# An E-Branchformer layer, forward and backward, on one core: one instruction plan for the whole program in place of three, a new table of order offsets, and the last weight loads issued by another engine

## The chip, the cores and the metric

The kernel runs on one core of a Trainium2 chip. The metric is device time in microseconds (us), lower is better. The core's engines are TensorE (PE: matmuls, with PEld for loading the stationary operand), VectorE (DVE), ScalarE (ACT), GpSimd (POOL) and SyncE (SP), which here only issues DMA transfers. Each engine works through its own instructions in a fixed order and waits by semaphores where it needs another's result.

## The reference

One layer on x of shape (B, T, D) = (2, 4000, 144), and then its gradient with respect to all inputs; `_gelu` is the tanh form, `_layernorm` has no weights:

```python
    xa = _layernorm(x)
    q, k, v = split(xa @ w_qkv)
    p = softmax(q @ k.T * D ** -0.5)
    glob = (p @ v) @ w_att_out
    h = _gelu(xa @ w_mlp_in);  u, g = split(h);  g = _layernorm(g)
    gc = depthwise convolution of g over 5 time steps by dw_csgu
    loc = (u * gc) @ w_mlp_out
    m = concatenate([glob, loc]);  m = m + depthwise convolution of m over 5 time steps by dw_merge
    out = x + m @ w_merge
    # outputs: out, and the gradients of x, w_qkv, w_att_out, w_mlp_in, dw_csgu, w_mlp_out, dw_merge, w_merge for grad_out
```

Outputs are named `out_0` (the layer's result), `out_1` (the gradient of x) and `out_2` to `out_8` (of the weights).

## The kernel before

**Rows.** Nearly all of the time goes to attention, forward and backward at once, in `phase_att` (line 1525), called once per batch. A batch's 4000 tokens are 32 row blocks of 125. Below, "row" means such a block, 0 to 31 for the first batch and 32 to 63 for the second. For one row the steps are:

- `jit_mm`, `jit_tr` (lines 1574 to 1602): the row's queries and its output gradient, folded with the weights, are made by matmuls, copied to `qz` and transposed into `qt` by a DMA transpose (L1597).
- `quad` (from line 1606): scores **S** of the row against all 4000 tokens, and **dP** (gradient times values) for the row before it, in four quarters. A quarter has 128-row matmuls of 500 columns (L1615) and remainder matmuls with 16 rows (L1621), into PSUM tiles `ps`, of which there are two.
- `S_min` (VectorE, L1639): copy of the scores to `Pb` with the running extreme for the softmax; `P_exp` (ScalarE, L1647) the exponential; `P_tr` (L1651) one DMA transpose of the row's whole P, issued by SyncE, `SX<-Pb`.
- `PdP` (L1657, or L1660 and L1662): P times dP, into `SX`; `st_half` (L1844): its transpose in two DMA transposes by SyncE, `SX<-SX`.
- **Y** (`Y_half`, L1671): 32 matmuls from the transposed P into the row's attention result; **Z** (`Z_half`, L1717): 32 matmuls from the transposed P times dP. Both go to a PSUM tile `yz`, of which there is one. Y and Z are written to DRAM (`Yn_d`, `Zn_d`), and Z's row is transposed into `zt` (L1731).
- **X** (`X_group`, L1762): matmuls that add the parts for keys and values of all 32 blocks, two rows at a time, from `Pb` and `SX`; VectorE adds them up in `acc` (L1766, L1768).

For the last row of a batch the transposes are done by TensorE (`last_tr`, L1707). Between these steps lie the pieces of the local branch (`local_units`, line 450).

**Head.** Ahead of and inside the first two rows the class `Head` builds folded weights and `pre_pieces` the normalised input `xa_aug` and its transpose `xaT_m`; its `rstd` is a power on GpSimd (L399), and the taps of the depthwise convolutions are multiplied out on GpSimd (L236). A tile of zeros is written to DRAM (`zdram`) to fill padding.

**Boundaries.** At the end of a batch the class `Merge` loads `go_h` and `Yg` (L2003, L2004, L2017, L2018 and the helper lines 41 and 42), and runs the merge branch's matmuls `Hmm` (`Hps`, L2053). The first boundary, between the batches, lies near 540 to 590 us of the profile, the second, before the weights' gradients (class `Final`), near 1150 to 1220.

**Weights for the end.** `end_weights` (line 98) loads the weights that `Final` and the last steps of `Merge` use into a space where the data `goT` and `xaT_m` were. Its DMAs are issued by GpSimd; it is called after the second batch's rows, and the planner places its loads where the space is free.

**What sets the order.** The program is written in source order. The class `Planner` (line 1104) then orders each engine's instructions by a simulated list schedule. Each instruction group has a key: its place in the source plus an offset from the table `LEAD`, which is looked up by its class (the step's tag, the engine, the tile's name, as in `H15t P` or `e_gn D.rsr`). At each simulated moment the ready group with the lowest key is taken, no further than 700 instructions ahead of the oldest that is left. Costs of instructions and DMAs are formulas in `cost` and `plan`. `plan` is called three times: twice from `phase_att`, when t reaches the last row of a batch, and at the end. So the order of each engine is three plans, one after the other: nothing crosses a cut.

Of the kernel before, what the change touches and what calls it, by code (L numbers as in the profile page):

```python
# [14 lines left out]
D = 144  # L15
# [82 lines left out]
def end_weights(k, W, pool):  # L98
    eng = k.nc.gpsimd
    W.Wqkv = load_k_(k, pool, k.w_qkv, 0, 3 * D, "Wqkv_e", eng)  # L100
    W.Wo = load_k_(k, pool, k.w_att_out, 0, D, "Wo_e", eng)
    W.Wm = [load_k_(k, pool, k.w_merge, h * D, D, "Wm_e%d" % h, eng) for h in range(2)]
    W.Wl = load_k_(k, pool, k.w_mlp_out, 0, D, "Wl_e", eng)
    W.Wvo = unspill(k, pool, W.Wvo_d, "Wvo_e", eng)
    W.sWm = [unspill(k, pool, W.sWm_d[h], "sWm_e%d" % h, eng) for h in range(2)]
    W.sWr = [unspill(k, pool, W.sWr_d[h], "sWr_e%d" % h, eng) for h in range(2)]


class Head:
# [18 lines left out]
    def loads(self):  # L128

        k, W, nc, wp, wt = self.k, self.W, self.k.nc, self.k.wpool, self.wt  # L130
        k.PL.tag("hl")
# [313 lines left out]
U0 = 1  # L445

# [251 lines left out]
Fdwct A.Pb:-15251 D.Pb:-13343 D.jf:1333 P:-5943 S.out_5_dram:-14635  # L698
Fdwit A.Pb:2718 D.Pb:-11748 P:-17532 S.out_4_dram:-14282
Fdwm0t A.Pb:-15906 D.Pb:-5467 D.dwma:-18911 D.jf:-15667 P:-12424 S.out_8_dram:-19182  # L700
Fdwm1t A.Pb:-19065 D.Pb:-16718 D.dwma:-19949 D.jf:-17808 P:-13749 S.out_7_dram:-14976 S.out_8_dram:-17102
Fdwvt A.Pb:-12429 P:-17392 P.Pb:-11874 S.out_2_dram:-13890 S.out_3_dram:-20599
Fdwxt A.Pb:-11921 P:-16236 P.Pb:-16679 S.out_6_dram:-16186
Fhbt A.Pb:-16772
Fht0t A.Pb:-15071 P:-16732 P.Pb:-15290
Fht1t A.Pb:-5982 P:-13475 P.Pb:-6001
Fqkt A.Pb:-5046 D.Pb:1780 P:-19513 P.Pb:-14575 S.out_2_dram:-12213
Fweightst A.Pb:2012 A.R:-11583 D.R:-12504 P:-16671 P.Pb:4074
H0d P:3856
H0t P:2300  # L710
H10d P:3336
H10t P:1535
H11d P:1114
H11t P:-15701
H12d P:-577
H12t P:-14835
H13d P:4246
H13t P:2042
H14d P:-996
H14t P:-12628  # L720
H15d P:-2292
H15t P:-19983
H1d P:1355
H1t P:-18472
H2d P:-10611
H2t P:-11591
H3d P:-2204
H3t P:2819
H4d P:-3689
H4t P:-15136  # L730
H5d P:-11610
H5t P:-16462
H6t P:-17582
H7d P:143
H7t P:2736
H8d P:1402
H8t P:4559
H9d P:-828
H9t P:-10610
clrh D.qz:121  # L740
da0d D.dx_s:1989 D.pj:1819
da0t D.dx_s:-19356 D.pj:4366
da1d D.dx_s:1833 D.pj:-2064
da1t D.dx_s:1450 D.pj:380
da2d D.dx_s:-1184 D.pj:-11591
da2t D.dx_s:-16872 D.pj:-16742
da3d D.dx_s:-9926 D.pj:2641
da3t D.dx_s:1738 D.pj:-14783
da4d D.dx_s:2120 D.pj:-10584
da4t D.dx_s:-14598 D.pj:-13576  # L750
da5d D.dx_s:1764 D.pj:-2040
da5t D.dx_s:-17958 D.pj:-15842
da6d D.dx_s:-26 D.pj:-4981
da6t D.dx_s:-17014 D.pj:167
da7d D.dx_s:-809 D.pj:-1508
da7t D.dx_s:-13863 D.pj:-17458
db0d A.t:1488 D.dx_c:-2255 D.t:-10855 P.Pb:-9933 S.out_1_dram:3805
db0t A.t:-15437 D.dx_c:-4986 D.t:-16936 P.Pb:-14840 S.out_1_dram:-11860
db1d A.t:8260 D.dx_c:593 D.t:-10761 P.Pb:-450 S.out_1_dram:-763
db1t A.t:-14235 D.dx_c:-14619 D.t:-14824 P.Pb:-18556 S.out_1_dram:-4816  # L760
db2d A.t:-10051 D.dx_c:-346 D.t:-1051 P.Pb:1345 S.out_1_dram:-10878
db2t A.t:-14314 D.dx_c:2973 D.t:-14455 P.Pb:-16686 S.out_1_dram:-15013
db3d A.t:-2311 D.dx_c:-12078 D.t:-256 P.Pb:4162 S.out_1_dram:-5923
db3t A.t:5187 D.dx_c:1471 D.t:-14832 P.Pb:-14659 S.out_1_dram:-14078
db4d A.t:700 D.dx_c:-5966 D.t:1978 P.Pb:5255 S.out_1_dram:-1006
db4t A.t:2357 D.dx_c:-15418 D.t:-17568 P.Pb:-16684 S.out_1_dram:3764
db5d A.t:7691 D.dx_c:1168 D.t:3548 P.Pb:4528 S.out_1_dram:1494
db5t A.t:-13237 D.dx_c:-12298 D.t:2401 P.Pb:-18508 S.out_1_dram:-14515
db6d A.t:-1202 D.dx_c:143 D.t:-2913 P.Pb:6516 S.out_1_dram:-1989
db6t A.t:992 D.dx_c:-905 D.t:-16578 P.Pb:-11985 S.out_1_dram:-12231  # L770
db7d A.t:-1326 D.dx_c:-2082 D.t:-2907 P.Pb:-1548 S.out_1_dram:-5951
db7t A.t:3489 D.dx_c:1682 D.t:-12820 P.Pb:-19955 S.out_1_dram:-13857
dgn_un D.c:-1050 D.l_gc:1027 D.nc:-45 P:6418 P.l_w:-5741
dhT_un S.dhT:-9892
dmd A.A_dM1T:3192 P:-1498
dmt D.A_dM1T:-13970 P:1403
dug_un A.dugr:-3801 P:-11295
dug_une A.dugr:3554 P:1368
dug_unh A.dugr:-1398 P:3647
dwc_un0 A.l_fl:-590 P:1255 P.A_dwc:4666  # L780
dwc_un1 A.l_fl:1673 P:-1034 P.A_dwc:4861
dwi_un A.l_fl:-979 P:3938 P.A_dWiT:-5316
e_dgc D.gd:1399 P.gd_rem:-11587 S.gd:-1599
e_dgce D.gd:-3413 P.gd_rem:-4142 S.gd:1142
e_dgch D.gd:1199 P.gd_rem:-11746 S.gd:6998
e_dh D.dhr:-1092 D.l_dd:-12499
e_du D.l_dd:6397
e_gn D.rsr:-2328 P.gd:-3884
e_gne D.rsr:-79 P.gd:7432
e_gnh D.rsr:-303 P.gd:-161  # L790
e_gp D.gpr:3201 D.l_sq:2314
e_gpe D.gpr:-3362 D.l_sq:2278
e_h D.l_hg:1917 P.l_q:-6726
e_he D.l_hg:1135 P.l_q:8342
e_hh D.l_hg:1742 P.l_q:544
e_m D.l_z:6720 P.l_th:-4350
e_me D.l_z:5526 P.l_th:-114
e_mh D.l_z:543 P.l_th:-52
e_stat D.mv:589 D.st:-39 D.ve:-938 P.rsr:1338 P.ur:5433
e_state D.mv:-314 D.st:1383 D.ve:1372 P.rsr:-178 P.ur:-10200  # L800
e_stath D.mv:1805 D.st:-408 D.ve:-4106 P.rsr:-5732 P.ur:-252
e_tanh A.l_th:-10935 D.l_z:-1255 P.l_a:1563
e_tanhe A.l_th:1202 D.l_z:3963 P.l_a:-377
e_tanhh A.l_th:76 D.l_z:406 P.l_a:595
ehd D.Hs:7635 S.H_d:-597
eht D.A_H:-15626
ex0 A.Pb:-2362
ex0d A.Pb:-310
ex0e A.Pb:-2899
ex0h A.Pb:2136  # L810
ex0t A.Pb:-13483
ex1 A.Pb:2211
ex1d A.Pb:-10370
ex1e A.Pb:-931
ex1h A.Pb:-499
ex1t A.Pb:-17638
ex2 A.Pb:2132
ex2d A.Pb:6419
ex2e A.Pb:222
ex2h A.Pb:997  # L820
ex2t A.Pb:2723
ex3 A.Pb:2425
ex3d A.Pb:1449 P:-9919
ex3e A.Pb:-2552
ex3h A.Pb:-9641
ex3t A.Pb:-45 P:-11409
gc_uni A.l_gc:3754 D.ugr:-1884 P:5596 S.ug_d:-6345
gm0d A.goT:-10916 P:-1170
gm0h A.goT:-5942 P:535
gm1d A.goT:-628 P:3264  # L830
gm1h A.goT:-408 P:-942
gm2d A.goT:-1090 P:3249
gm2h A.goT:-7899 P:3264
gm3d A.goT:-466 P:-2130
gm3h A.goT:1016 P:-5787
gmad A.goT:-10233 P:-2750
gmah A.goT:-12011 P:-621
gmbd A.goT:3435 P:-2104
gmbh A.goT:-171 P:-3462
grd P.go_r:3222  # L840
grh P.go_r:-209
gs0d D.R:-4545 P:1256
gs0h D.R:15 P:1219
gs1d D.R:-2449 P:313
gs1h D.R:-12605 P:-10337
gs2d D.R:440 P:-6571
gs2h D.R:950 P:817
gs3d D.R:-1058 P:-835
gs3h D.R:2954 P:-4366
hRh D.R:-4194  # L850
hah P.A_dWiT:-973 P.A_dwc:-11699
# [5 lines left out]
hm1h A.Q:1240 A.RW:127 A.SX:2039 P:4414  # L857
hm1th A.M1T:-8007 P:4192
hoh P.xa_aug:-1937
htapr0h P.SX:1965  # L860
htapr1h P.SX:-1414
htp00h A.SX:-2503
htp10h P.SX:2191
# [1769 lines left out]
```

## Time and profile before

| | us |
|---|---|
| median of 3 runs | 1293.33 (1292.07 to 1297.97) |
| the profiled execution | 1294.54, with a span of 1292.8 |
| mean granted clock of TensorE | 0.996 |
| TensorE busy | 1243.4 (96%) |
| VectorE busy | 1050.1 (81%) |
| ScalarE busy | 756.4 (59%) |
| GpSimd busy | 502.4 (39%) |

The profile's page gives each engine's busy time, the chain that ended last, the costliest groups of instructions with their mean durations, and the DMA queues; busy time of PE comes from modelled ends. The trace behind it was also asked for the busy time by windows, for what an engine waited for, and for the order in time at single places. In such rows `SPq` is SyncE's time for issuing a transfer, and a line such as `DMA SX<-SX` in the chain is a transfer from its issue to its landing.

### The profile page before, as it was taken

How to read it: one execution, taken by the hardware profiler on the slowest of the kernel's cores; microseconds unless marked ns; L12 is line 12 of the kernel's file. 1: busy time of each engine (PE TensorE's matmuls, PEld its weight loads, DVE VectorE, ACT ScalarE, POOL GpSimd, SP SyncE). 2: the span in 40 equal slices, each digit the busy share in tenths (PEclk: the TensorE clock that was granted, in tenths of full speed). 3: DMA queues.
4: the chain of work that ended last, by engine and by line, in shares of the span. 5: the costliest groups of instructions: out<-in, count | busy, mean ns of one | idle time of the engine just before them, and what ended most of it. 6: DMA issues, size and time to landing. Idle time of an engine off the chain costs nothing.

```text
span 1292.8 us, 38682 instructions
## 1 busy us (share of the span) xinstructions
PE 1243.4 (96%) x15698; PEld 1024.7 (79%) x15698; DVE 1050.1 (81%) x2824; ACT 756.4 (59%) x1232; POOL 502.4 (39%) x987
## 2 busy tenths in 40 slices
PE   6999999999999999989899999999999999998998
PEld 3578888888788888879787878888888888886997
DVE  7599888989898988668868988888889798876655
ACT  4766666665666566443846656666666666553382
POOL 7553434334434433313634444444444343331111
PEclk9999999999999999999999999999999999999999
DMA  3588988898889898794259998999799898999612
GB/s 101 105 159 156 161 156 154 142 166 150 155 146 153 154 163 150 135 219 113 67 108 171 152 150 158 163 154 160 136 144 169 150 157 149 168 152 154 158 27 84
DMA packets 631017, 186.50 MB, mean 144 GB/s; under 512 B 611651, under 2 KB 625766, under 8 KB 630832
## 3 DMA queue, kind: packets, MB, share of 16 engines
q1 hardware_dynamic: 629490, 182.39, 78.1%
q8 instruction: 122, 2.00, 0.6%
q0 software_dynamic: 800, 1.44, 0.5%
q14 instruction: 57, 0.47, 0.1%
q10 hardware_dynamic: 548, 0.21, 0.1%
HBM read 20.82 MB, written 14.22 MB: 27 GB/s over the span
## 4 chain that ended last, share of the span: by engine, by line
PE 79%; DMA 8%; DVE 7%; ACT 2%; POOL 2%; issue 1%; SPq 0%; DVEq 0%; POOLq 0%; ACTq 0%
PE X L1762 20%; PE ps L1615 15%; PE yz L1717 10%; PE yz L1671 8%; PE ps L1621 7%; DMA SX<-SX 3%; PE po L2150 2%; PE Hps L2053 2%; DMA SX<-Pb 1%; PE pj L1578 1%; PE pc L581 1%; PE pd L529 1%; PE pd L596 1%; PE pw L641 1%; DMA qt<-qz 1%
## 5 line engine op out<-in xcount | busy, mean ns | idle before, releaser
L1639 DVE TENSOR_SCALAR_CACHE_REDUCE Pb<-ps 125x1000 bf16<-125x1000 f32 x256 | 306.3, 1197 | 74.5 <-PE ps L1621 71.8
L1647 ACT ACTIVATE Pb<-Pb,nm 125x1000 bf16<-125x1000 bf16 x256 | 279.0, 1128 | 119.1 <-DVE nm L1641 118.4
L1762 PE MATMUL X<-SX 125*125 125x144 bf16 x2048 | 294.8, 229 | 2.1 <-ACT l_fl L623 1.9
L1762 PE MATMUL X<-SX,Pb 125*125 125x144 bf16 x2048 | 290.0, 226 | 0.0
L1762 PEld LDWEIGHTS <-SX 125*125 125x125 bf16 x2048 | 259.1, 137 | 28.4 <-issue 28.4
L1660 ACT CAST SX<-ps 125x1000 bf16<-125x1000 f32 x189 | 188.1, 995 | 152.8 <-PE ps L1621 149.2
L1615 PE MATMUL ps<-xaT_m,qt 128*125 128x500 bf16 x1024 | 264.1, 378 | 3.5 <-DMA qt<-qz 1.9
L1762 PEld LDWEIGHTS <-Pb 125*125 125x125 bf16 x2048 | 260.5, 137 | 3.1 <-issue 3.1
L1768 DVE TENSOR_TENSOR acc<-X,acc 125x432 f32<-125x432 f32 x372 | 200.5, 551 | 37.3 <-PE X L1762 34.9
L1717 PE MATMUL yz<-xa_aug,SX 125*125 125x144 bf16 x2048 | 153.5, 230 | 10.9 <-DMA SX<-SX 8.2
L1615 PEld LDWEIGHTS <-qt 128*125 128x125 bf16 x1024 | 122.1, 138 | 43.7 <-issue 2.7
L1717 PEld LDWEIGHTS <-SX 125*125 125x125 bf16 x2048 | 141.2, 139 | 19.1 <-DMA SX<-SX 9.5
L1671 PE MATMUL yz<-xa_aug,SX 125*125 125x145 bf16 x2048 | 142.0, 227 | 1.8 <-DMA SX<-Pb 1.8
L1671 PEld LDWEIGHTS <-SX 125*125 125x125 bf16 x2048 | 135.1, 137 | 3.6 <-DMA SX<-Pb 2.5
L1662 DVE TENSOR_TENSOR SX<-SX,Pb 125x1024 bf16<-125x1024 bf16 x189 | 131.5, 696 | 4.2 <-ACT SX L1660 4.0
L1621 PEld LDWEIGHTS <-qt 16*125 16x125 bf16 x1024 | 37.0, 129 | 102.0 <-issue 102.0
L1621 PE MATMUL ps<-XR,qt 16*125 16x500 bf16 x1016 | 112.2, 421 | 0.0
L1657 DVE TENSOR_TENSOR SX<-ps,Pb 125x1000 bf16<-125x1000 f32 x67 | 80.1, 1195 | 7.9 <-PE ps L1621 6.6
L1695 POOL TENSOR_SCALAR SX<-qz,rl 125x144 bf16<-125x144 bf16 x62 | 25.5, 412 | 146.2 <-DVE rl L1677 123.8
L624 POOL TENSOR_TENSOR A_dwc<-l_fl,A_dwc 128x512 f32<-128x512 f32 (+2 forms) x48 | 38.5, 801 | 102.6 <-ACT l_fl L623 102.4
L499 POOL TENSOR_SCALAR l_a<-l_sq 125x576 bf16<-125x576 bf16 x32 | 22.3, 696 | 106.7 <-ACT l_sq L497 106.4
L2053 PE MATMUL Hps<-Yg,go_h 125*128 125x144 bf16 x640 | 53.8, 226 | 1.7 <-DMA Yg<-ug_d 1.7
(498 smaller groups left out, 2293.7 us busy)
## 6 DMA issues: line engine op xcount, KB each, us to landing
Yn_d<-yn SPq DMA_DIRECT2D x64, 35.2 KB
Zn_d<-qz SPq DMA_DIRECT2D x64, 35.2 KB
ug_d<-ugr SPq DMA_DIRECT2D x32, 70.3 KB
SX<-in_x_dram SPq DMA_DIRECT2D x16, 140.6 KB
out_dram<-Pb SPq DMA_DIRECT2D x16, 140.6 KB
out_dram<-SX SPq DMA_DIRECT2D x16, 140.6 KB
Pb<-in_grad_out_dram SPq DMA_DIRECT2D x8, 252.0 KB
go_h<-in_grad_out_dram SPq DMA_DIRECT2D x4, 504.0 KB
```

The costliest lines, as they stand in the source:

```text
L1615: mm = nc.tensor.matmul(pp[r // 2][:, r % 2, 0:CH], QT[i][:, 3 * h, 0:PB], xaTm[:, c * CH:(c + 1) * CH], start=True, stop=False)
L1621: nc.tensor.matmul(pp[r // 2][:, r % 2, 0:CH], QT[i][rs, 1 + h, 0:PB], xr, start=False, stop=True)
L1639: nc.vector.tensor_scalar(pv(Pbuf, i % NPB, c2), src, -1.0, 3.0e38, op0=ALU.mult, op1=ALU.min, accum_out=NM[i][:, c2:c2 + 1])
L1647: nc.scalar.activation(v, v, ACT.Exp, bias=NM[i][:, 4:5], scale=-1.0)
L1657: nc.vector.tensor_tensor(pv(Sbuf, i % NDB, c2), src, pv(Pbuf, i % NPB, c2), op=ALU.mult)
L1660: nc.scalar.copy(pv(Sbuf, i % NDB, c2), src)
L1662: nc.vector.tensor_tensor(sc, sc, pchunk(i % NPB, c2), op=ALU.mult)
L1671: nc.tensor.matmul(Y, PT[0:PB, j, 0:PB], xaa[:, j, 0:D + 1], start=(j == 0), stop=(j == NB - 1))
L1717: nc.tensor.matmul(Z, ST[0:PB, j, 0:PB], xaa[:, j, 0:D], start=(j == 0), stop=(j == NB - 1))
L1762: nc.tensor.matmul(X[:, jj, :], l, r, start=(n_ == 0), stop=(n_ == len(ops) - 1))
L1768: nc.vector.tensor_tensor(av, X[:, 0:nj, :], av, op=ALU.add)
L2053: nc.tensor.matmul(H[a // 6][0:rows, a // 3 % 2, (a % 3) * D:(a % 3 + 1) * D], lhs, self.src[h][:, 2 + j, :], start=(j == 0 and a % 3 == 0 ...
```

## The change

- `plan` is called once, at the end, over the whole program. The two calls in `phase_att` are gone.
- The table `LEAD` of some 400 lines is replaced by another of the same kind and size, for all classes.
- The planner's model: a matmul group that starts before 36 us (`COLD`) takes twice its time; a reduction is costed by its input; a VectorE memset has a cost of its own; DMAs move 2.5e5 bytes per us and not 2.6e5; after issuing a transpose, SyncE is taken as busy until 2.2 us before its end; a tile's first use constrains the order but not as a data dependency. Warm-up matmuls can be planned, but their number is 0.
- `end_weights` is split. Its first 11 DMAs (`Wqkv`, `Wo`, `Wm`, `Wl`, `Wvo`) are issued by SyncE, and called at t = 24 of the second batch; the last four (`sWm`, `sWr`, now `end_taps`) by SyncE at the place where all of them were called before.
- The zeros for `zdram` are set by VectorE and not by GpSimd, and earlier.

The matmuls are the same 15698 and the computation is the same. Outside the table the diff is, cut to its core:

```diff
 def end_weights(k, W, pool):
-    eng = k.nc.gpsimd
+    eng = k.nc.sync
     W.Wqkv = load_k_(k, pool, k.w_qkv, 0, 3 * D, "Wqkv_e", eng)
...
     W.Wvo = unspill(k, pool, W.Wvo_d, "Wvo_e", eng)
+
+
+def end_taps(k, W, pool):
+    eng = k.nc.sync
     W.sWm = [unspill(k, pool, W.sWm_d[h], "sWm_e%d" % h, eng) for h in range(2)]
...
     def loads(self):
...
+        k.PL.tag("warm")
+        zt = self.zt = wt(4, [128, 16 * k.NB])
+        nc.vector.memset(zt, 0.0)
...
+COLD = 36.0
+WARM = 0
...
 LEAD = {}
 for _s in """
-Fdwct A.Pb:-15251 D.Pb:-13343 D.jf:1333 P:-5943 S.out_5_dram:-14635
...
     def cost(self, e, ins):
...
+        if "Reduce" in kind:
+            n = max(n, self.count(aps_i[0]))
...
+            if kind == "InstMemset":
+                d = 0.07 + n / (1150.0 if aps_o[0].bass_ap.tensor.dtype == F32 else 2300.0)
...
                     if born.get(t.name, g) != g:
-                        preds[g].add(born[t.name])
+                        after[g].add(born[t.name])
...
-                    g["tr"] = n * 2 / 2.6e5
+                    g["tr"] = n * 2 / 2.5e5
...
-                    w = max(0.0, port_t - s) if G["port"] else 0.0
+                    w = max(0.0, port_t - s) if G["port"] else G["d"] if e == "PE" and s < COLD else 0.0
...
                     free_t[e] = s + w + G["d"]
+                    if e == "SP" and G["d"] > 1:
+                        free_t[e] = max(free_t[e], end - 2.2)
...
-def phase_att(k, W, b, S, A, M, head=None, late=None):
+def phase_att(k, W, b, S, A, M, head=None, late=None, extra=None):
...
             if t == NB - 1:
-                PL.plan(k.plan_from, PL.mark())
-                k.plan_from = PL.mark()
                 PL.mode = "dt"[b]
...
+            if extra and t == 24:
+                PL.tag("lv")
+                extra()
...
     def clear():
...
-        zt = hd.wt(4, [128, 16 * NB])
-        nc.gpsimd.memset(zt, 0.0)
-        nc.gpsimd.dma_start(k.zdram[:, :].rearrange("a (b c) -> (a b) c", c=16 * NB), zt)
+        nc.gpsimd.dma_start(k.zdram[:, :].rearrange("a (b c) -> (a b) c", c=16 * NB), hd.zt)
...
+    ew = Arena([goT, xaT_m])
+    phase_att(k, W, 1, SS[1], A, M, late=[lambda g=g: M0.out_g(g) for g in range(k.NG)], extra=lambda: end_weights(k, W, ew))
...
-    end_weights(k, W, Arena([goT, xaT_m]))
+    end_taps(k, W, ew)
```

More of the change, by code (lines that the diff above doesn't have):

```diff
@@ new lines @@
+Fweightst A.Pb:6938 A.R:-18371 D.R:-16365 P:-4821 P.Pb:-16719
+H0d P:2392
+H0t P:6178
+H10d P:3725
+H10t P:1442
+H11d P:6647
+H11t P:5670
+H12d P:-1923
+H12t P:-4748
+H13d P:-1362
+H13t P:1079
+H14d P:-5896
+H14t P:3029
+H15d P:467
+H15t P:7068
+H1d P:3102
+H1t P:3097
+H2d P:1224
+H2t P:-11399
+H3d P:2882
+H3t P:-2501
+H4d P:2781
+H4t P:-2718
+H5d P:-13497
+H5t P:6574
+H6d P:-2474
+H6t P:1071
+H7d P:2374
+H7t P:-4808
+H8d P:-13489
+H8t P:285
+H9d P:-13056
+H9t P:-208
+clrh D.qz:2897
+da0d D.dx_s:3417 D.pj:1967
```

780 lines of the change are left out of this document (375 added, 405 removed).

## The prediction

> **What bounds the kernel now.** I read the page first (parts 1 and 4), then busy time by window of 20 us, then the waits of TensorE and, at the worst places, the chain, SyncE's timeline and the clock in windows of 2 us.
>
> ```profile
> PE 1243.4 (96%) x15698; PEld 1024.7 (79%) x15698; DVE 1050.1 (81%) x2824; ACT 756.4 (59%) x1232; POOL 502.4 (39%) x987
> PE 79%; DMA 8%; DVE 7%; ACT 2%; POOL 2%; issue 1%; SPq 0%; DVEq 0%; POOLq 0%; ACTq 0%
> ```
>
> TensorE is busy 96% and carries 79% of the chain. The number of matmuls does not change (15698), so the change can only win what TensorE loses. I count that loss with TensorE's own paces: each kind of matmul at its median start-to-start time (0.211 us for a 500-column step, 1.50 for 24 of L1762, 2.03 for 32 of L1671). All matmuls sum to 1212 us. The first starts at 7.4, the last ends near 1287, and the span is 1292.8 with 6.2 us of tail. Between lie 1279 us, so some 67 us are lost to idle time and to half pace. The windows show where (columns: length, then each engine's busy time and instructions, granted clock, DMA share, GB/s):
>
> ```profile
> 20.00:40.00 20.00, 19.14 (x89) 9.13 (x88) 11.22 (x21) 7.84 (x17) 14.62 (x42) 1.00 0.19 61
> ...
> 560.00:580.00 20.00, 17.47 (x253) 15.71 (x250) 13.34 (x29) 11.29 (x15) 3.17 (x7) 1.00 1.01 230
> ...
> 680.00:700.00 20.00, 17.40 (x190) 12.73 (x188) 18.16 (x45) 13.59 (x24) 11.65 (x23) 1.00 1.00 163
> 1040.00:1060.00 20.00, 20.00 (x252) 16.26 (x250) 17.85 (x51) 13.21 (x21) 9.11 (x17) 1.00 1.01 160
> ...
> 1180.00:1200.00 20.00, 14.82 (x198) 13.86 (x195) 8.89 (x16) 8.20 (x12) 1.64 (x4) 0.91 1.09 173
> ```
>
> Steady rows, like 1040 to 1060, lose nothing. The losses by my count of paces are: 0 to 40, 13 beyond the start; 60 to 80, 3.7; the first boundary, 540 to 580, 8.0; 620 to 700, 9.1; 740 to 760, 2.9; the second boundary, 1150 to 1220, 11.5. The rest is spread thin. What TensorE waits for at those places (total, times, longest):
>
> ```profile
> PE yz L1717 <- DMA SX<-SX: 8.2, 6, 4.4
> ...
> PE yz L1671 <- DMA SX<-Pb: 1.8, 2, 1.5
> PE Hps L2053 <- DMA Yg<-ug_d: 1.7, 1, 1.7
> ```
>
> All are transfers issued by SyncE. The worst is in the chain near the second boundary, and SyncE's timeline says why:
>
> ```profile
> 1179.08 0.27 SPq L2003 DMA_DIRECT2D go_h<-in_grad_out_dram  x1
> 1179.46 3.66 SPq L1844 DMA_TRANSPOSE SX<-SX  x1
> ```
> ```profile
> 1179.46 13.96 DMA SX<-SX
> ```
>
> The second-half transpose of row 62 goes out just behind the first bulk load of the merge stage and among the rest; it took 14 us where its issue is typically 2.1 and Z follows 5 us after the issue in other rows. TensorE then stood for 4.39 us ahead of its 16 matmuls of L1717, and came back at half pace:
>
> ```profile
> 1194.00:1196.00 2.00, 2.00 (x20) 2.00 (x19) 0.37 (x1) 0.00 (x0) 0.00 (x0) 0.50 1.09 218
> 1196.00:1198.00 2.00, 2.00 (x28) 2.00 (x27) 0.69 (x1) 1.30 (x2) 0.00 (x0) 0.74 0.93 154
> ```
>
> The clock column sums to 1.7 us lost there ((1-0.91)+(1-0.50)+(1-0.74) of 2 us each), and to 1.7 again at 544 to 550, after stops of 0.6 and 1.15 us. So a stop has two prices.
>
> **The change, part by part.** I compare the order of every engine before and after, and give distances in microseconds of TensorE work at the paces above; the distance from S to Y of a row is the work between its last score matmul and its first Y matmul.
>
> *First boundary.* The single plan lets row 30's and 31's steps mix across the old cut. SyncE issues both last transposes and the reads of x ahead of the merge loads (before, go_h at 548.6 went ahead of row 30's P transpose at 551.9), Z29 comes later and the quads of row 31 are spread; the merge matmuls (L2053) start at 546.5 us of work instead of 537.7, where they waited 1.74 us for Yg. Of 8.0 lost, the wait for Yg, the stops before X and Z29 and their half pace go (1.7+0.6+1.15+1.7=5.2); Z30 gets 1.6 to 3.0 of new risk. I take -4, bounds -5.5 to -1.
>
> *Rows 33 to 37 (680 to 760).* The second half of Z33, which stood for 1.99 us at 698, lies 2.5 us of work later; the Zn write and zt transpose that stood ahead of P's transpose at 747.8 on SyncE (Y then waited 1.50) lie behind it. These two stops are 3.5 us: -3.5, bounds -5 (what follows them late goes as well) to 0.
>
> *Second boundary.* Row 62's transpose now has one 70 KB load and one Yn write ahead of it; all go_h loads lie behind Zn of row 62, the last of the bulk. The stop (4.39), its half pace (1.7) and the 0.86 ahead of it go, 7 in all. Late next: the merge matmuls, at 1136 us of work, near 1199 on the clock; some 3.4 MB at the 218 to 236 GB/s of these windows take 15 us from 1181, landing at 1196, so 0 to 3 comes back. I take -6, bounds -8 to -2. Other thin places: -1, bounds -2 to +1.
>
> *Weights for the end on SyncE.* Eleven loads now stand, in SyncE's queue, between a half transpose of row 54 and the P transpose of row 55. An issue of this kind costs 0.31 to 0.42 us on SyncE, so 4 to 5 us. Queued behind: P transpose of 55, on which Y55 waits, and the following half transposes, on which Z waits. From the end of S to the P transpose took 5.6 us at best and 8.0 at the median, from there to Y 8.2 and 10.7; with the block it is 10+8.5=18.5. TensorE's work between S and Y of this row is 15.6, so a stop of up to 2.9 there, and 0.5 to 3 at the next rows, where the distance falls to 13.3 (was 17.3). I take +3, bounds +1 to +6. The window 1040 to 1060 above is where it falls; it had no loss to hide it. What GpSimd saves there is nothing: no wait on its weight loads is in the list. The four tap loads at the end are far ahead of their use: 0. Rows 0 to 31: row 10's distance falls from 18.3 to 14.3: +1, bounds 0 to +2.4.
>
> *Head.* The memset of the padding source moves from GpSimd to VectorE (one instruction, about 1 us beside DMA waits), so the padding lands early; that removes P transpose 0's old 13 us wait. But the plan puts eight tap multiplies and the mask that waits for ten tap loads between GpSimd's `rstd` operations (1.63 to 1.68 us each): by hand, the last rstd ends at 26.5 to 28 instead of 25.3, the last xa_aug at 30 instead of 27, so row 0's S ends at 35 to 36 instead of 32.4, its transpose goes at 41 and Y0 can start at 49 to 50; the order puts Y0 at a place that TensorE reaches near 45, and Z0's distance falls from 8.6 to 6.6. Planned double cost to 36 us fits the steps, slow until 39:
>
> ```profile
> 38.95 1.04 PE L1615 MATMUL ps<-xaT_m,qt 128*125 128x500 bf16 x2
> ...
> 40.54 0.59 PE L1615 MATMUL ps<-xaT_m,qt 128*125 128x500 bf16 x2
> ```
>
> I take +3 (part of the wait is filled by work moved forward), bounds -2 to +5.
>
> TensorE had run without a gap from 27.9, so the switch came 11 us after that. The Trainium skill ("TensorE: Matmul & The Clock Gate", section "Part 1: The HAM clock gate") says that full speed follows about 3.4 us of sustained activity. The stops at 1189 agree (1.7 us lost is 3.4 at half); the head does not, so the measured 39 decides, and by the page's 3.4 the head would be fast from 31.3 and cost some 4 us less, before and after alike.
>
> *Tail.* The last chain is another output's, with as many steps: 0, bounds -1 to +1.
>
> Sum: -4-3.5-6-1+3+1+3 = -7.5 on the profiled 1294.5, that is 1287.0. That execution lies 1.2 over the median, so 1286.
>
> **Rivals.** *Larger gain, 1277.* Most terms at their good ends: -5.5-5-8-1+1+0-2 = -20.5 is the limit, -16 a fair case. For it: each of the three places had one cause, and it is moved out of the way. Against: SyncE already spends 751 us, 58% of the span, issuing transposes (62 of 4.99 us, 124 of 2.09, 152 of about 1.2), and the head's GpSimd chain is longer.
>
> *Gains given back, 1294.* The head stays at half pace until TensorE's supply is unbroken, 11 us after Y0: from 41 to 61, of which 4 are idle, half of 16 is +8, and -7.5+8 is no change. For it: clock rows after both stops; the old switch came late. Against: nothing in the old head shows a return to half pace after 40.5 in spite of gaps at 44 to 52.
>
> *Slower, 1301: the P transpose's chain becomes the bound in steady rows.* The median distance from S to Y falls from 18.3 to 17.7, while the chain's median is 8.0+10.7=18.7. Where the queue cannot catch up, 25 of the 40 rows whose order differs lose 0.6: +15 on 1286. It decides where the distance is under what the chain takes under load. For it: DMA share 0.9 to 1.0 in those rows. Against: at best the chain takes 13.8, and in the trace Y waited 1.8 us in all.
>
> **How the numbers follow.** Chances: forecast 0.40 (own range 1281 to 1291), larger gain 0.20 (1272 to 1281), given back 0.22 (1291 to 1298), slower 0.18 (1298 to 1308). A measurement tells 0.5%, 6.5 us, from no change: below 1286.9 is faster. Just over half of the forecast and all of the larger gain make 0.43; the rest of the forecast and the given-back case 0.39; slower 0.18. The range 1275 to 1301 leaves out the lower third of the one side and half of the slower case.
>
> **What would show it.** Right: no stop over 1 us before Z62 and clock 1.00 at 1180 to 1200; Hps no longer waiting for Yg near 578; Y55 or a neighbour waiting 1 to 3 us for SX<-Pb near 1040; row 0's S ending after 34 and a stop before Y0. Wrong: `yz L1671 <- DMA SX<-Pb` over 10 us in all (slower), 500-column steps at 0.42 beyond 48 us (given back), or stops of more than 3 us at either boundary for go_h.

## The result and the profile after: slower by 1.1 to 1.3%

| | before | after |
|---|---|---|
| median beside each other | 1292.70 us | 1309.97 us (1307.42 to 1315.44, 4 runs) |
| ratio of the runs, 95% interval | | 1.0132 (1.0089 to 1.0176) |
| the same again in a later test (10 runs) | | 1.0105 (1.0078 to 1.0132) |
| profiled execution, its span | 1294.54, 1292.8 | 1310.46, 1308.5 |
| mean granted clock of the profiled execution | 0.996 | 0.987 |
| the same over all runs, with the tests below | 0.990 (105 runs) | 0.989 (14 runs) |

The forecast was 1286; the change made the kernel about 14 to 17 us slower. Executions of one kernel lie up to 17 us apart here, in part because TensorE spends a different time at half pace in each, so verdicts below are ratios from several runs. The two profiled executions differ in the clock, the two kernels over their runs do not: the profile of before is one with little half pace. (The clock record of an execution begins with its first change of clock, so these means leave out the slow start ahead of it.)

The page's first and fourth parts of the changed kernel. Lines 1525 and up of before stand some 20 lines further down (L1615 is L1635, L1671 is L1691, L1717 is L1737, L1762 is L1782, L2053 is L2075).

```profile
PE 1252.5 (96%) x15698; PEld 1029.8 (79%) x15698; DVE 1053.7 (81%) x2825; ACT 756.4 (58%) x1232; POOL 492.8 (38%) x971
...
PE 72%; DVE 11%; DMA 7%; ACT 5%; issue 2%; POOL 1%; SPq 1%; ACTq 0%; DVEq 0%; POOLq 0%
```

TensorE's share of the chain fell from 79% to 72%, and VectorE and ScalarE rose from 9% to 16%, while transfers stayed at 7 to 8%. The windows of 20 us (the same columns as in the prediction), first three of the kernel before that the prediction does not show, then the changed kernel:

```profile
40.00:60.00 20.00, 17.30 (x193) 12.61 (x193) 10.01 (x19) 18.46 (x36) 8.86 (x26) 1.00 0.55 92
60.00:80.00 20.00, 17.92 (x192) 13.20 (x189) 17.89 (x43) 12.82 (x26) 9.87 (x19) 1.00 0.88 151
600.00:620.00 20.00, 20.00 (x337) 20.00 (x335) 19.97 (x112) 14.79 (x21) 9.32 (x12) 1.00 0.02 7
```
```profile
20.00:40.00 20.00, 15.76 (x87) 8.52 (x87) 15.39 (x40) 10.61 (x17) 13.44 (x27) 0.96 0.27 85
40.00:60.00 20.00, 15.44 (x154) 13.46 (x153) 4.75 (x11) 13.82 (x30) 10.46 (x37) 0.67 0.56 106
60.00:80.00 20.00, 19.39 (x120) 11.27 (x119) 8.84 (x20) 9.98 (x25) 5.31 (x9) 0.60 0.33 67
560.00:580.00 20.00, 19.43 (x244) 15.89 (x241) 14.22 (x30) 5.91 (x10) 6.44 (x16) 1.00 0.99 174
600.00:620.00 20.00, 15.41 (x237) 14.73 (x236) 16.47 (x76) 1.14 (x2) 2.92 (x6) 1.00 0.77 210
1060.00:1080.00 20.00, 17.63 (x192) 13.07 (x190) 17.52 (x40) 11.22 (x18) 6.00 (x11) 0.99 0.84 143
1180.00:1200.00 20.00, 20.00 (x264) 16.92 (x261) 15.69 (x36) 10.60 (x16) 7.29 (x16) 1.00 0.86 136
```

The window 1180 to 1200 is full (14.82 busy before): the second boundary did what was forecast. At 560 to 580 the stops are gone too, but 600 to 620 has new ones. At 1060 to 1080 rows that ran without a gap now have gaps. In the head the granted clock is 0.67 and 0.60 from 40 to 80 us, where this execution of before has 1.00. (Ahead of the first change of clock, at 39.9 us in before and 31.6 in the changed kernel, the column reads 1.00 though TensorE is at half pace: 500-column steps take 0.42 us there, and 0.21 behind it.)

To set the kernels side by side I add up the time lost against TensorE's paces by stretches of TensorE work (the count of the prediction: clock time less work done). One execution each:

```
work done, us      0-100  100-500  500-600  600-750  750-950  950-1050  1050-1150   rest   sum
before              26.7      7.3     11.7      9.5      4.0       1.9       12.9    0.8   74.8
after               41.1     11.5     11.4      7.0      4.7       8.3        5.2    1.8   91.0
e5_after            36.0     11.5     11.8      6.5      4.9       9.6        6.2    1.8   88.3
e1_head             32.5      9.2     10.2      6.7      4.5       8.2        4.9    1.7   77.9
e2_cold0            35.9      8.8     12.0      6.7      4.4       9.6        6.2    1.8   85.4
e3_gp               35.0     11.5     11.3      6.6      4.7       9.4        8.0    1.8   88.3
e4_oneplan          26.1      8.1     14.3      9.5      4.3       1.9       11.4    0.8   76.4
e7_edges            27.3      7.2     14.3     10.6      3.9       3.9        2.8    1.9   71.9
e8_edges_gp         32.6      7.3     16.7      8.3      3.9       1.9        4.3    1.8   76.8
e10_cut1            29.5      7.8     14.4      9.0      4.3       4.0        3.3    1.9   74.2
e13_cut1gp          26.7      7.5     12.7      8.7      3.8       2.0        4.2    1.8   67.4
e14_sp              43.1      7.7     17.7      5.8      9.0       7.3        3.4    1.8   95.8
e15_sp_cold0        42.6      7.9     18.8      5.3      9.3       4.7        3.2    1.9   93.7
```

So the 16.2 us of this pair of profiles are +14.4 in the head, +4.2 in the first batch's rows, -0.3 at the first boundary, -2.5 behind it, +0.7, +6.4 in rows 54 to 57, -7.7 at the second boundary, and +1.0 at the end.

The head's entry scatters with the execution. Up to 100 us of work TensorE's order in e4_oneplan, e7_edges, e8_edges_gp, e10_cut1 and e13_cut1gp is that of before, but for 8 of 1101 matmuls at most, and these six profiles lost 26.1 to 32.6 us, 28.2 in the mean. The three with the order of the changed kernel (after, e5_after, e3_gp) lost 35.0 to 41.1, 37.4 in the mean. So the new head costs about 9 us, and the 14.4 of the first pair is in part luck of the pair.

### The profile page after: what moved, and what is told of

Same layout as the page of the kernel before. It is cut to its first block, busy times and chain, and to the rows that moved or that the text cites. A ratio compares the mean times of both kernels' runs of the same rounds, so it can differ in the third digit from the quotient of the medians.

```text
span 1308.5 us, 38626 instructions
## 1 busy us (share of the span) xinstructions
PE 1252.5 (96%) x15698; PEld 1029.8 (79%) x15698; DVE 1053.7 (81%) x2825; ACT 756.4 (58%) x1232; POOL 492.8 (38%) x971
## 4 chain that ended last, share of the span: by engine, by line
PE 72%; DVE 11%; DMA 7%; ACT 5%; issue 2%; POOL 1%; SPq 1%; ACTq 0%; DVEq 0%; POOLq 0%
PE X L1782 17%; PE ps L1635 14%; PE yz L1737 8%; PE yz L1691 8%; PE ps L1641 6%; DVE Pb L1659 3%; PE po L2172 2%; ACT Pb L1667 2%; DMA Yg<-Yn_d 2%; PE Hps L2075 2%; DVE acc L1788 1%; PE pw L653 1%; DVE SX L1677 1%; DMA Pb<-in_grad_out_dram 1%; PE pj L1598 1%
## 5 line engine op out<-in xcount | busy, mean ns | idle before, releaser
L1782 PE MATMUL X<-SX 125*125 125x144 bf16 x2048 | 294.5, 229 | 3.1 <-DVE acc L1786 1.3
L1782 PE MATMUL X<-SX,Pb 125*125 125x144 bf16 x2048 | 288.9, 226 | 0.9 <-POOL SX L1719 0.9
L1782 PEld LDWEIGHTS <-SX 125*125 125x125 bf16 x2048 | 258.9, 137 | 29.2 <-issue 28.8
L1635 PE MATMUL ps<-xaT_m,qt 128*125 128x500 bf16 x1024 | 265.8, 379 | 7.1 <-DVE Pb L1659 4.0
L1782 PEld LDWEIGHTS <-Pb 125*125 125x125 bf16 x2048 | 260.1, 137 | 3.7 <-issue 3.5
L1635 PEld LDWEIGHTS <-qt 128*125 128x125 bf16 x1024 | 122.9, 138 | 49.5 <-issue 9.4
L1737 PE MATMUL yz<-xa_aug,SX 125*125 125x144 bf16 x2048 | 150.8, 228 | 3.9 <-ACT ty L1707 3.6
L1737 PEld LDWEIGHTS <-SX 125*125 125x125 bf16 x2048 | 139.8, 138 | 10.8 <-issue 9.4
L1691 PE MATMUL yz<-xa_aug,SX 125*125 125x145 bf16 x2048 | 144.7, 229 | 0.6 <-DMA SX<-Pb 0.2
L1691 PEld LDWEIGHTS <-SX 125*125 125x125 bf16 x2048 | 137.5, 138 | 3.9 <-issue 3.2
L618 POOL TENSOR_SCALAR l_w<-gd,nc,c 125x144 f32<-125x144 bf16 x64 | 31.2, 496 | 92.5 <-DVE c L616 92.2
```

The costliest lines, as they stand in the source:

```text
L1635: mm = nc.tensor.matmul(pp[r // 2][:, r % 2, 0:CH], QT[i][:, 3 * h, 0:PB], xaTm[:, c * CH:(c + 1) * CH], start=True, stop=False)
L1691: nc.tensor.matmul(Y, PT[0:PB, j, 0:PB], xaa[:, j, 0:D + 1], start=(j == 0), stop=(j == NB - 1))
L1737: nc.tensor.matmul(Z, ST[0:PB, j, 0:PB], xaa[:, j, 0:D], start=(j == 0), stop=(j == NB - 1))
L1782: nc.tensor.matmul(X[:, jj, :], l, r, start=(n_ == 0), stop=(n_ == len(ops) - 1))
```

## The experiments

**First test: which part of the change loses.** Theory A: the head, whose new order has two half-pace stretches. Rival B: the head costs the forecast 3 to 5 us and the rest is lost in the rows, by the weights on SyncE or the new table.

*e1_head*, the old head's offsets in the changed kernel (TensorE's order in the head comes near that of before but is not the same: the two differ from the 39th matmul on):

```diff
-COLD = 36.0
+COLD = 0.0
 LEAD: entries of the head's classes (tags that end in the head's h) as in the kernel before
```

> The changed kernel with the head of the kernel before: the table's offsets of the head's classes are those of before, and COLD is 0; from 250 us of TensorE work on, the order is that of the changed kernel. Theory A (the head's new order loses some 14 us, through two stretches at half pace): 1310-14 = 1294 to 1299, mean clock 0.994 or more. Rival B (the head is no more than the forecast 3 to 5 us, the rest is lost in the rows): 1305 or more.

Measured: 1.0035 (1.0004 to 1.0067). At before's 1293 that is 1297 us: the head, with the rows up to 250 us of work whose order follows from it, carries 0.7 to 1.0%, some 9 to 12 us. Theory A holds for the place. That half pace is the reason is not shown by this test, and the mean clock of its ten runs was 0.992, not 0.994.

*e2_cold0*, the changed kernel with `COLD = 0.0` alone:

> The changed kernel with COLD = 0 and nothing else: TensorE is planned at full rate in the head, with the new offsets; the order after 250 us of work stays. If planning at half rate is what spoils the head (it lets the plan put all of row 1's quads right behind row 0's): 1295 to 1300. If the new offsets do it whatever the rate: 1307 to 1312.

Measured: 1.0037 (1.0008 to 1.0065), 1297 to 1298 us. So the order that comes of planning TensorE at half pace carries the loss, with the new offsets as they are; this is by the ratio alone. Its profile lost 35.9 us up to 100 us of work, more than e1_head's 32.5 and as much as e5_after below, with as much idle time of TensorE (20.1 us). What the trace shows in its favour is 2.7 us in the rows from 100 to 500; and the mean clock of its ten runs was 0.994, against 0.990 in 24 runs of the changed kernel's head, which is some 5 us. The same edit made on e14_sp (e15_sp_cold0 below) won only 0.24%, with intervals that overlap.

*e3_gp*, the weights for the end on GpSimd as before:

```diff
-    eng = k.nc.sync
+    eng = k.nc.gpsimd
...
-    phase_att(..., extra=lambda: end_weights(k, W, ew))
+    phase_att(...)
...
+    end_weights(k, W, ew)
     end_taps(k, W, ew)
```

> The changed kernel with the weights for the end issued by GpSimd at the end of the source, as before; TensorE's order is the same to within 0.1 us of work in rows 0 to 60. If the eleven loads in SyncE's queue cause the loss at rows 54 to 57 (6.2 us): 1303 to 1305 and no stop there. If it is TensorE's order there (two rows' quads without work between): 1308 to 1312, with the same stops.

Measured: 1.0099 (1.0065 to 1.0133), some 1305.5 us at before's 1293 and so between the two expectations, and 9.4 us lost at rows 54 to 57: the stops stay. There the queue is not the cause, in this order. What is, the waits of TensorE in the changed kernel between 1060 and 1100 us say (total, times, longest):

```profile
PE ps L1635 <- DVE Pb L1659: 1.5, 2, 1.3
PE yz L1737 <- ACT ty L1707: 1.4, 1, 1.4
PE ps L1635 <- DVE nm L1661: 0.5, 1, 0.5
```

Row 56's last quad and row 57's first stand side by side at 997.7 and 999.0 us of work (993.6 and 998.4 before). With two PSUM tiles of scores the second waits for VectorE to empty the first, and Z of row 55 comes straight behind Y, whose result ScalarE must first scale. Counted against TensorE's paces the stops are 1.37, 0.69 and 1.57 us, and 1.7 us of half pace follow (clock 0.64 from 1080 to 1084, 0.94 ahead of it).

*e4_oneplan*, the kernel before with one plan: the two calls of `plan` in `phase_att` removed, nothing else.

> The kernel before with one plan over the whole program in place of three; table, costs, head and weights as before, so only the places around the two old cuts differ. If the cuts themselves cost something there: 1287 to 1291. If the gain at the boundaries in the changed kernel comes from the new offsets: 1292 to 1295.

Measured: 0.9990 (0.9966 to 1.0013). The cuts by themselves cost nothing; the gain at the second boundary comes from the new offsets (11.4 us lost there with one plan and the old ones, 5.2 with the new). No run separates the offsets from the planner's new line on a tile's first use, which every kernel with the gain has too.

**Second test: half pace, and the boundary's gain by itself.**

*e5_after*, the changed kernel unedited.

> The changed kernel again, with nothing edited, beside the others and the kernel before. Theory A puts its loss at 10 us or more over the earlier test with the old head (ratio 1.0035): 1.011 to 1.015 here, and another pattern of half-pace stretches in the head, since the same order in the test with the weights on GpSimd had 17.9 us less of them after the first 40 us. Rival B (the order's waits alone): the head's loss at 100 us of work is again 41 to within 1.

Measured: 1.0105 (1.0078 to 1.0132). This is just under theory A's range, and 9 us over e1_head where 10 or more were expected. The head lost 36.0 us here and 41.1 in the first profile, with the same order, so its loss varies, and the order's waits are not all of it, as rival B had it. The two profiles differ in the time at half pace up to 100 us, 45.5 and 57.4 us (counted from the first matmul to the first full-pace record, and then by the clock). TensorE's idle time after its first matmul, up to 105 us, is 20 to 22 us in all three profiles of this order, against 10.1 before. These waits are the one thing that separates the two heads in every profile: 9.0 to 10.1 us in the six with the order of before, 20.3 to 22.3 in the three with the new one. Half pace does not separate them. Up to 100 us the six show 31 to 48 us of it, and before's own 32.5 is near the low end; the three show 40 to 57. A stretch of half pace in which TensorE waits anyway costs nothing, so what counts is the work that TensorE does in it, each us of which costs one more: 16.7 to 26.3 us in the six (20.0 in the mean), 17.6 to 26.4 in the three (21.7). The waits in the changed kernel's first 95 us, and below them those of before:

```profile
PE pt L427 <- ACT xa_aug L418: 5.1, 2, 2.6
PE hps L180 <- DMA Pb<-in_w_qkv_dram: 4.9, 1, 4.9
PE pt L427 <- POOL xa_aug L422: 3.6, 2, 2.8
PE hps L267 <- ACT VUT L268: 3.1, 1, 3.1
```
```profile
PE hps L170 <- POOL ident L27: 7.4, 1, 7.4
PE pt L417 <- ACT xa_aug L408: 0.5, 1, 0.5
PE pt L417 <- POOL xa_aug L412: 0.4, 1, 0.4
PE pt L382 <- ACT VUT L258: 0.2, 1, 0.2
```

The line with `in_w_qkv` and that with `ident` are the time ahead of TensorE's first matmul, which comes 2.5 us earlier in the changed kernel. Behind it the waits for `xa_aug` are 8.6 us and were 0.9, and that for `VUT` is 3.1 and was 0.2; all of these end before Y of row 0 begins, at 48.9 us.

*e6_warm150*, the changed kernel with `WARM = 150`.

> The changed kernel with 150 matmuls on zeros (290 columns each), which the planner places where TensorE would stand idle, all ahead of Y of row 0. If half pace is what the head loses, and idle TensorE is what brings it: full pace from before 20 us and none of the half pace near 40 to 52, so 4 to 8 us less than the changed kernel. If the waits for VectorE, ScalarE and the loads set the head: the same or up to 3 us more.

Measured: 1.0078 (1.0051 to 1.0105) beside 1.0105 for e5_after, 3.5 us less, short of the 4 to 8 expected, and the intervals overlap. Half pace up to 100 us fell from 45.5 to 17.0 us, yet row 3's Y began at 115.0 us and not at 115.8: Y of row 0 waits for the last of the 150 and began at 65.2 instead of 50.1 us. Inconclusive for the size of the loss, since the cure delays the head as much as it helps.

*e7_edges*, the kernel before with the new offsets at the boundaries alone:

```diff
 LEAD: entries of before; of the changed kernel only for the two boundaries, the end, and the weights
 def end_weights, end_taps, phase_att(extra=...): as in the changed kernel
-                PL.plan(k.plan_from, PL.mark())
-                k.plan_from = PL.mark()
...
-                        preds[g].add(born[t.name])
+                        (after if g > len(groups) // 2 else preds)[g].add(born[t.name])
```

> The kernel before with one plan, with the new offsets only for the classes of the two boundaries and the end, with the weights issued by SyncE, and with a tile's first use as an order constraint in the second half of the program; TensorE's order in the head and the rows is that of before to 0.1 us of work, that around the second boundary and the end that of the changed kernel to 0.9. Theory: the changed kernel's gain at the second boundary (12.8 lost becomes 5.2) stands alone once head and rows 54 to 57 are taken back: ratio 0.991 to 0.996, some 1284 to 1288. Rival: what is won at the boundary is given back at the end: 0.998 to 1.002.

Measured: 0.9981 (0.9957 to 1.0006). The second boundary's loss fell from 12.9 to 2.8 us, as forecast; but the first boundary and what follows rose from 21.2 (500 to 750) to 24.9. Little of that is shown to come from the new offsets there: with TensorE's order of before up to 750 us, e10_cut1 lost 23.4 and e13_cut1gp 21.4, and with one plan and the old offsets e4_oneplan lost 23.8. The ratio lies at the edge of the rival's range, its interval reaches into the theory's, and rows 54 to 57 lost 3.9 where before lost 1.9.

*e8_edges_gp*, the same with the weights on GpSimd.

> The same as e7_edges with the weights for the end issued by GpSimd at the end of the source, as before. If the move to SyncE helps at the second boundary (there the test with GpSimd lost 2.8 us more than the changed kernel between 1100 and 1150 us of work): 2 to 3 us slower than e7_edges, with the extra stop at the second boundary. If the weights do not matter: the same.

Measured: 0.9986 (0.9959 to 1.0013), the same in all. In its parts it is not: 1.9 lost at rows 54 to 57 (e7_edges 3.9), 4.3 at the second boundary (2.8; one execution each).

**Third test: what keeps the clock down.** In the changed kernel TensorE ran almost without a gap (0.6 us in all) and yet at half pace from 59 to 76 us. Windows of 4 us (clock is the third number from the end):

```profile
60.00:64.00 4.00, 4.00 (x12) 1.10 (x10) 1.15 (x2) 1.47 (x4) 0.00 (x0) 0.50 0.00 0
64.00:68.00 4.00, 3.96 (x17) 1.98 (x16) 2.07 (x4) 2.34 (x6) 0.00 (x0) 0.50 0.61 113
68.00:72.00 4.00, 3.46 (x25) 2.76 (x24) 1.38 (x3) 2.22 (x6) 2.93 (x6) 0.50 0.73 137
72.00:76.00 4.00, 4.00 (x16) 1.70 (x16) 1.54 (x2) 0.94 (x3) 0.47 (x1) 0.50 0.14 34
```

Over the first 110 us of the 14 profiles up to e12_warm150, I added up the columns of the matmuls that begin in each 3.41 us of the clock's grid, each weighted by the share of the array's rows and columns that it fills. At half pace, at 0.42 us for 500 columns, some 4080 fit. The clock opened after 32 such windows, 31 of which held 2956 or more; it stayed at half after 121, none with over 3041. With the three later profiles it is 40 windows (39 with 2956 or more) and 160 (two over 3041, at 3089 and 3444). Where a matmul that runs across an edge is shared between its two windows, all 160 hold 2980 or less and 39 of the 40 hold 2962 or more; the one exception is the window ahead of 39.9 us in before. TensorE was busy for 95% or more of 49 of the 160, so time busy alone does not open the clock. From 59 to 73 us TensorE mostly runs quads of rows 0 and 1, 1000 full columns and 1000 with 16 rows of 128; these four windows held 2059 to 2988, and the fifth, after which the clock opened, 3149.

*e9_fat*, the remainder matmuls of these rows with 128 rows:

```diff
+                    if fat:
+                        m2 = nc.tensor.matmul(pp[r // 2][:, r % 2, 0:CH], QT[i][:, 3 * h, 0:PB], xaTm[:, c * CH:(c + 1) * CH], start=False, stop=True)
+                        PL.fat.add(m2.ins.name)
+                        continue
                     nc.tensor.matmul(pp[r // 2][:, r % 2, 0:CH], QT[i][rs, 1 + h, 0:PB], xr, start=False, stop=True)
...
-                        S_min(t, s, quad(S_work(t, s), t > 0)[0])
+                        S_min(t, s, quad(S_work(t, s), t > 0, True)[0])
...
-                        PdP(0, s - 4, quad(dP_work(0, s - 4))[0], s % 2 == 1)
+                        PdP(0, s - 4, quad(dP_work(0, s - 4), True, True)[0], s % 2 == 1)
```

> The changed kernel, where the remainder matmuls of rows 0 and 1 in the head have 128 rows in place of 16 (they repeat the main matmul, so these rows' scores are not the layer's); number, columns and, but for 16 matmuls, the order on TensorE are the same. Theory from the traces: the clock opens when 3.41 us hold some 3000 columns' worth of filled array, which at half pace (4096 at most) a run of quads with 16-row remainders does not reach (2950). Then full pace from 32 to 36 us at the latest with at most two half-pace stretches of 3.4 to 6.8 us up to 80 us, and 3 to 7 us less than the changed kernel (ratio 1.004 to 1.008). If rows don't count, only time busy: 24 to 31 us of half pace between 32 and 80 again, ratio 1.010 to 1.012.

Measured: 1.0063 (1.0039 to 1.0087), within the theory's range and some 5 us under e5_after's 1.0105, though the two intervals overlap a little. The same windows of e9_fat:

```profile
60.00:64.00 4.00, 3.18 (x25) 2.21 (x23) 2.92 (x4) 3.16 (x9) 0.67 (x1) 1.00 0.47 88
64.00:68.00 4.00, 3.51 (x32) 2.14 (x33) 1.59 (x4) 1.69 (x5) 2.99 (x6) 1.00 1.02 195
...
72.00:76.00 4.00, 4.00 (x44) 3.09 (x43) 2.62 (x8) 2.35 (x6) 1.50 (x4) 1.00 0.29 83
```

The clock opened at 28.9 us and closed only from 42.5 to 49.4, 31.4 us at half in all, with 11.6 us of work done in it, less than in any of the nine profiles above. TensorE is idle as long as in the changed kernel (24.1 up to 105 us), and row 3's Y begins at 113.0 us: 2 to 8 us ahead of the three profiles of the changed head (114.8, 115.8, 120.9), which fits the half pace that is gone, and still behind all six profiles of the old head's order (105.0 to 111.5), with the waits left. So a fuller array would have helped the changed head; that the old head was better fed is not shown.

*e10_cut1*, a version from these results: e7_edges with the first boundary as before (its cut and its offsets kept, and the line on a tile's first use applied behind that cut).

```diff
+                if b == 0:
+                    PL.plan(k.plan_from, PL.mark())
+                    k.plan_from = PL.mark()
```

> The kernel before with the first cut kept (two plans): head, rows and first boundary in the order of before; the new offsets only for the second boundary and the end, weights issued by SyncE. Theory: of e7_edges' terms the second boundary's gain (10 us) stays and the first boundary's loss (5 us) goes: ratio 0.991 to 0.995, 1283 to 1288. If boundary gains are lost to the clock or the end: 0.997 to 1.000.

Measured: 0.9969 (0.9948 to 0.9990), faster than both kernels, though short of the theory's 0.991 to 0.995 and just under the other range: of 9.6 us that its profile won at the second boundary, 2.1 went at rows 54 to 57 and 1.1 at the end, and this execution lost 2.8 more in the head and 2.7 more from 500 to 600, in both of which TensorE's order is that of before (in the head but for 8 matmuls).

*e11_warm60* and *e12_warm150*, e10_cut1 with `WARM = 60` and `WARM = 150`.

> e10_cut1 with up to 60 matmuls on zeros where the plan finds TensorE idle ahead of Y of row 0, planned at full rate; the zeros are set by VectorE. Theory: the clock opens before 12 us; half pace up to 60 us falls from 32 us to under 20; 2 to 6 us less than e10_cut1. If the head's waits set its length: the same to within 2 us.

> e11_warm60 with 150 of them. Theory: still less half pace, but each costs 0.12 to 0.24 us of TensorE ahead of Y0: between 2 us less and 3 us more than e11_warm60.

Measured: 1.0033 (1.0005 to 1.0062) and 0.9988 (0.9966 to 1.0010), both not better than e10_cut1. e11_warm60 is 8 us slower and e12_warm150 nearly 6 us faster than e11_warm60, neither of which was expected. Half pace up to 100 us fell to 20.6 and 13.0 us (39.8 in e10_cut1), but row 3's Y began at 110.9 and 114.0 us and not at 108.4. The first theory fails: with half pace mostly gone the head is not shorter. That its own waits, and the dummies ahead of Y0, then set its length is how I read it; no run separates the two.

**Fourth test: what was open at rows 54 to 57.**

*e13_cut1gp*, e10_cut1 with the weights on GpSimd.

> e10_cut1 with the weights for the end issued by GpSimd at the end of the source. In the kernels with the order of before in the rows, those with the eleven loads on SyncE lost 4.0 us (both of them) between 950 and 1050 us of work, the two with GpSimd 1.8 and 1.9. Theory (the loads hold up P's transpose of row 55): 1.8 to 2.0 here, and 1 to 2 us more lost at the second boundary than in e10_cut1; in all the same to 2 us less (ratio 0.994 to 0.998). If the loads cost nothing: 4 us lost there here too.

Measured: 0.9970 (0.9945 to 0.9994), with 2.0 us lost at rows 54 to 57, as the theory had it, and 4.2 at the second boundary, 0.9 more than e10_cut1. In all the two are alike. Where the order of before is kept, the eleven loads on SyncE do hold up Y. TensorE's only waits there were, in e10_cut1 (1020 to 1100 us; its L1676 is Y) and in e13_cut1gp (1010 to 1090; its L1717 is Z):

```profile
PE yz L1676 <- DMA SX<-Pb: 2.0, 2, 1.1
```
```profile
PE yz L1717 <- DMA SX<-SX: 0.2, 1, 0.2
```

*e14_sp*, the changed kernel without the planner's new line on SyncE:

```diff
-                    if e == "SP" and G["d"] > 1:
-                        free_t[e] = max(free_t[e], end - 2.2)
```

> The changed kernel without the planner's line that keeps SyncE busy after a transpose; all else the same. It moves row 55's first quad from 974.1 back to 966.9 us of work (966.8 before) and the last of row 56 and the first of row 57 apart; at the first boundary it puts three quads of row 31 side by side. Theory: the loss between 950 and 1050 falls from 8 to 10 us to 4 or less, 3 us come back at the first boundary; ratio 1.005 to 1.009. If the order there is not the cause: 8 to 10 us stay and the ratio is 1.010 or more.

*e15_sp_cold0*, the same with `COLD = 0.0` too.

> e14_sp with COLD = 0 as well: both assumptions of the planner taken back, the table, the single plan and the weights on SyncE kept. Theory: the two carry the whole loss; ratio 0.996 to 1.002. If the new table is worse of itself: 1.004 or more.

Measured: 1.0136 (1.0084 to 1.0188) and 1.0112 (1.0072 to 1.0151). The theory falls. The line does place row 55 as it did, but without it 7.3 and 4.7 us are still lost at rows 54 to 57: Y of row 54 now waits for the transfer that the loads hold up,

```profile
PE yz L1689 <- DMA SX<-Pb: 2.3, 1, 2.3
PE yz L1735 <- ACT ty L1705: 1.4, 1, 1.4
```

(waits of e14_sp, 1050 to 1100 us), and Z of 55 still comes straight behind its Y. New stops appear elsewhere: 6 to 7 us more at the first boundary and 4 to 5 between 750 and 950. The new table and the planner's assumptions depend on each other; taking one back moves the loss. Their heads also lost some 7 us more than e5_after's, with 60 to 63 us at half pace, though e14_sp has TensorE's order of the changed kernel there.

## Why the prediction was wrong, step by step

Between the forecast of -7.5 us and the +16.2 of the first pair of profiles lie 23.7 us: 11.4 in the head, 3.7 at the first boundary, 3.4 at rows 54 to 57, 3.2 in rows 0 to 31, and 2.0 in all the rest.

**What bounds the kernel, and the second boundary: right.** The loss there fell by 7.7 us in the first pair of profiles and by 6.7 in the second (-6 forecast, bounds -8 to -2), the long stop and its half pace are gone, and by e4_oneplan it is not the missing cut that does it but the new offsets, with the line on a tile's first use.

**Rows 33 to 37: right.** From 600 to 750 us of work 2.5 to 3.0 us were won (-3.5 forecast).

**First boundary: the size failed.** The old stops at 540 to 580 went, but 500 to 600 lost 11.4 and 11.8 us against 11.7 (-4 forecast, bounds -5.5 to -1). The new order moves the merge loads behind the transposes, and I counted only what that frees. What came late next was those loads:

```profile
PE Hps L2075 <- DMA go_h<-in_grad_out_dram: 3.0, 1, 3.0
PE pm L1988 <- DMA Yg<-Yn_d: 1.2, 1, 1.2
```

(waits of the changed kernel, 590 to 640 us). At the second boundary I had worked out when the bulk lands; here I had not.

**Weights on SyncE: a price that another loss hid.** The loads cost 2.0 us where the order of before is kept (e10_cut1 against e13_cut1gp), near the +3 forecast. In the changed kernel rows 54 to 57 lost 6.4 to 7.7 us more, and not by them (e3_gp): two quads side by side and Z straight behind Y. I had listed the falling distance from S to Y there, but priced it as a wait for the transpose; the spacing of quads, which have two PSUM tiles, was the thing to look at. "What GpSimd saves there is nothing" was wrong: with the loads on GpSimd the second boundary lost 0.9 us (e13_cut1gp, e10_cut1), 1.5 (e8_edges_gp, e7_edges) and 1.8 to 2.8 us more (e3_gp, the two profiles of the changed kernel). Two executions of one order differ by 1.0 there, so it is the sign, the same in all three, that counts.

**Head: the step that decided.** +3 was forecast, with +5 as the upper bound; 8 to 14 us were measured against the one profile of before, 9 between the means of three profiles and of six. The step that failed is this term: I followed one chain (GpSimd's rstd through `xa_aug` to Y0), priced only the stop that its end makes ahead of Y0, and took off "part of the wait" as filled by work moved forward. The waits lie all along the head and were not filled. TensorE's idle time behind its first matmul rose from 9 to 10 us in all six profiles of the old head's order to 20 to 22 in all three of the new, in the first profile 8.6 of it for `xa_aug` between 9 and 25 us (0.9 before) and 3.1 for `VUT` up to 46.5 (0.2); 2.5 us come back by an earlier start. Y0 itself came at 48.9 us, as forecast at 49 to 50 and 8 us earlier than in before (56.9). The price shows behind it: row 1's Y was at 73 to 79 us (73.1), row 2's at 99 to 105 (90.5). Why TensorE met these waits, the order of GpSimd's work or its own, no run separates.

Half pace I had as the rival that gives the gains back, with 0.22 and +8 us. Its sign, 500-column steps at 0.42 us beyond 48 us, came true from 59 to 76 us. But the argument against it, that the old head shows no return to half pace, held only for the one execution I had: four of the five other profiles of that order show it, in e8_edges_gp up to 65 us. Half pace costs both heads some 20 us, so the rival had the price of a stretch right and not what the change adds. "Planned double cost to 36 us fits the steps" took the clock as given by time; by e9_fat it is given by the work. The old head's late switch at 39.9 us, behind 12 us without a gap, was the hint that time busy does not decide.

**Other rows.** +1 was forecast for rows 0 to 31, bounds to +2.4; 4.2 us were lost, 3.4 of them in four stops of 0.45 to 1.26 us at rows 6, 10, 12 and 13. With other heads (e1_head, e2_cold0) it was 1.9 and 1.5: the plan of rows 2 to 12 follows from where the head leaves off. The slower rival (the P transpose's chain in steady rows) did not occur: `yz L1691 <- DMA SX<-Pb` is 0.2 us in all. (The 751 us of SyncE's issuing in the prediction was median times count; summed over the trace of before it is 811 us, 63% of the span, so the argument against the larger gain is a little stronger than it was put.)

**Left open.** Why the new offsets put the quads of rows 56 and 57 together: without the planner's line on SyncE the stops take another form, no more is shown. And why e2_cold0 is some 0.7% faster than the changed kernel while its profile shows as much idle time and half pace in the head.

## What to carry to other kernels

Where an order changes, price every wait of the engine that bounds the kernel, not only the one at the end of the chain that you follow, and take off for work that fills it only what is named and ready by then. Where a scheduler plans an engine whose pace depends on what it is fed, a pace that is fixed by time is a wrong model: check what the planned order itself does to the clock, and on several executions of both kernels, since one profile of before looked clean by luck. When stops at a stage are cured by moving transfers later, work out the landing of what was moved against its first reader at every such place. A gain by a search over a table holds for the whole plan: e13_cut1gp and e10_cut1, 0.3% faster than before, came from taking over the one stage whose gain the trace showed and leaving the rest in its old order.

## What the runs showed of the hardware that was not expected

- The granted clock follows how full the array is, and not only whether TensorE is busy: 17 us with 0.6 us of gaps ran at half pace (59 to 76 us), and the same matmuls with 128 rows in place of 16 ran at full pace. The step lies near 3000 full columns in 3.41 us in these profiles, of some 4080 that fit at half pace. For the way back there is no such step: from full pace the clock closed after windows that held up to some 3300 and stayed open with as few as 2670. The Trainium skill ("TensorE: Matmul & The Clock Gate", section "Part 1: The HAM clock gate") tells of the grid of 3.4 us and of two states, with which the records agree (all half-pace stretches between the first opening and the one that the end of the run cuts are multiples of 3.413 us). The sustained activity that the Trainium skill names there has to be read as filled array, by the 17 us above, which are five such windows.
- The same instructions in the same order spent 40 to 57 us of their first 100 at half pace in the changed kernel's head, and 31 to 48 us in that of before, depending on the execution.
